# Moving a transpose's transfers to ScalarE's queue, and four turns of the result to an earlier stage, in a fused attention and mixer kernel

## The chip, the cores and the metric

The kernel runs on one core of a Trainium2 chip. A core has five engines that run their own instruction streams: TensorE (PE, matrix products; PEld is its loading of weights), VectorE (DVE), ScalarE (ACT), GpSimd (POOL) and SyncE (SP), which here only issues transfers. An engine's stream is in order: an instruction that waits holds everything behind it on that engine. Transfers are issued from an engine's queue and carried out by 16 DMA engines that all queues of the core share. Engines work on SBUF (128 partitions), matrix products end in PSUM, inputs and outputs lie in DRAM.

The metric is the device time of one execution in microseconds (us), the median of several runs.

## What is computed

Attention with normalised queries and keys over 8 batches, 12 heads, 448 positions and 64 numbers a head, then a token mixer and a channel mixer over the 768 channels of the joined heads (`q`, `k`, `v` are of shape (8, 12, 448, 64), the result is (8, 448, 768), all in float32):

```python
def rmsnorm(x, g):
    return x / np.sqrt(np.mean(x * x, axis=-1, keepdims=True) + 1e-06) * g
scores = 1.0 / np.sqrt(64) * np.matmul(rmsnorm(q, g_q), rmsnorm(k, g_k).transpose(0, 1, 3, 2))
attn = np.exp(scores - np.max(scores, axis=-1, keepdims=True))
attn = attn / (np.sum(attn, axis=-1, keepdims=True) + 1e-09)
x = np.matmul(attn, v).transpose(0, 2, 1, 3).reshape(8, 448, 768)
...
h = np.maximum(x.transpose(0, 2, 1) @ w_tok1, 0.0) @ w_tok2     # 448 -> 256 -> 448, over positions
u = x + h.transpose(0, 2, 1)
return u + np.maximum(u @ w_ch1, 0.0) @ w_ch2                   # 768 -> 1536 -> 768, over channels
```

## The kernel before

**The order of work.** Everything is one long program. The order on PE, DVE, ACT and POOL is the order in which the code emits instructions (`manual_schedule`, L49). The work is cut into items, each with a cost in us and a function that emits it. `merge` (L27) interleaves lists of items in proportion to their costs; `run` (L120) emits them and adds each cost to a software clock. `later(us, fn)` (L116) puts a piece of work, always the issue of a transfer, into a list of pending work; `run` emits it once the clock has passed the time asked for. Pending work is emitted first in, first out. This clock only orders instructions: on the chip each still waits for what it needs.

**The stages of a batch.** The mixer of batch b is interleaved with the attention of batch b+1: scores on PE (L334), exponentials on ACT (L338), values on PE (L408). The attention leaves x channel by channel, in `uT` (6 chunks of 128 channels, 448 positions each). For batch b the mixer then runs

1. `x_items`: the token mixing needs positions on the partitions. From batch 1 on x is turned round through DRAM: DVE transposes the 32x32 blocks of a chunk (L615), `send_x` (L581) writes each half of x (3 chunks) to a scratch `xs` in DRAM with four transfers of 168 KB, and `load_x` (L589) reads it back with one of 672 KB. All are issued by SP. The first half's turn lies among the attention's items, the second half's among the last four double products of the batch before (`last`, L971).
2. `tok1` (L623): four products of half of the channels, each of four matmuls (L629), each followed by a ReLU on ACT (L632). `h` is 0 for the first half of x, 1 for the second.
3. `tok2` (L634): six products, one for each chunk (L637), that DVE adds to `uT` (L642). `moving_sums` (L650) then forms the differences that the channel mixing uses.
4. `ch1` (L749): 3 x 7 products (L761) with sums on DVE, POOL and ACT. This and the next stage form 2x2 block products from seven multiplications in place of eight.
5. `ch2` (L803) in two groups: "double" products, for chunks 0, 1, 3 and 4 (14 items), then in `last_items` (L889) seven "single" products for chunks 2 and 5, each of 12 matmul records in the trace (L818). ACT copies the first product (L831), DVE and POOL add the others to `uT`. Batch 0 uses plain products (`ch1_first`, `ch2_first`).

**Weights.** The channel weights stream in as units of 384 KB (L687), in six buffers, up to five ahead, from SP's queue. A double product needs two units, a single one.

**The result.** The finished `uT` holds channels on the partitions, so it is turned too. For each of six chunks `trans_y` (L852) transposes blocks on DVE into a tile `turned` (four buffers, `turn_pool`, L89), and `send_y` (L574) writes it with four transfers of 56 KB, issued by ACT. For all batches but the last, all six turns are put into the token mixing of the next batch: `left[:2]` beside the first two `tok1` items, `left[2:]` beside the other two and the `tok2` items (L958 and L959). In the last batch four turns lie beside the single products.

**Waits between transfers.** In the built program every transfer signals on one of eight semaphores, taken in rotation in program order across the queues, and an issue first waits until the previous transfer on its semaphore has landed. The profile shows this as waits of one queue for another queue's transfer.

Of the kernel before, what the change touches and what calls it, by code (L numbers as in the profile page):

```python
# [26 lines left out]
def merge(*lists):  # L27

    totals = [sum(c for c, _ in l) or 1.0 for l in lists]
    done = [0.0] * len(lists)  # L30
    at = [0] * len(lists)
    res = []
    while True:
        live = [i for i in range(len(lists)) if at[i] < len(lists[i])]
        if not live:
            return res
        i = min(live, key=lambda i: (done[i] + lists[i][at[i]][0] / 2) / totals[i])
        c, fn = lists[i][at[i]]
        at[i] += 1
        done[i] += c  # L40
        res.append((c, fn))
# [3 lines left out]
def whole(ctx, tc, shifted, pre, q, k, v, g_q, g_k, moe_w_tok1, moe_w_tok2, moe_w_ch1, moe_w_ch2, out):  # L45


    nc = tc.nc
# [13 lines left out]
    NC = C // P  # L62
# [4 lines left out]
    KC, KF = NC // 2, NF // 2  # L67
# [46 lines left out]
    clock, pending = [0.0], []  # L114

    def later(us, fn):  # L116

        pending.append((clock[0] + us, fn))

    def run(items):  # L120
        for c, fn in items:
            fn()
            clock[0] += c
            while pending and pending[0][0] <= clock[0]:
                pending.pop(0)[1]()
# [70 lines left out]
    def sum_items():  # L196


        def one(i):
            n = len(stages)  # L200
            if i < n:
                t = st["sum", i] = raw_tile()
                nc.sync.dma_start(out=eight(t)[:, 0:4], in_=slots(i, 0, 4))
            if 0 <= i - 2 < n:
                q = eight(st["sum", i - 2])
                nc.gpsimd.tensor_tensor(out=q[:, 6], in0=q[:, 1], in1=q[:, 0], op=ALU.subtract)
                nc.gpsimd.tensor_tensor(
                    out=q[:, 4:6], in0=q[:, 1:7:5], in1=q[:, 3:4].to_broadcast([P, 2, P]), op=ALU.add)
                nc.gpsimd.tensor_tensor(out=q[:, 7], in0=q[:, 2], in1=q[:, 5], op=ALU.subtract)
            if 0 <= i - 3 < n:  # L210
                nc.sync.dma_start(out=slots(i - 3, 4, 8), in_=eight(st.pop(("sum", i - 3)))[:, 4:8])
                st["summed"] = i - 3 if i - 3 < n - 1 else n
                load_units(st["at"])

        def eight(t):
            return t[:].rearrange("p n w -> p (n w)").bitcast(F32).rearrange("p (q n) -> p q n", q=NQ)
        return [(1.0, lambda i=i: one(i)) for i in range(len(stages) + 3)]
# [356 lines left out]
    def send_y(b, cc, t):  # L574
        dst = out[b][:, cc * P:(cc + 1) * P]
        for i in range(0, P, 32):
            nc.scalar.dma_start(  # L577
                out=dst[:, i:i + 32].rearrange("(n t) c -> t n c", t=32),
                in_=t[i:i + 32].rearrange("t (n c) -> t n c", c=32))

    def send_x(b, half, t):  # L581

        xs = st["xs"] = xs_pool.tile([KC * S, P], F32, name="xs")
        for i in range(0, P, 32):
            nc.sync.dma_start(
                out=xs[:, i:i + 32].rearrange("(n t) c -> t n c", t=32),
                in_=t[i:i + 32].rearrange("t (n c) -> t n c", c=32))

    def load_x(b, half):  # L589
        nc.sync.dma_start(  # L590
            out=x_tile(b, half)[0:R].rearrange("p j c n -> p (j c) n"),
            in_=st.pop("xs")[:].rearrange("(g p) n -> p g n", p=R))

    def x_tile(b, half):
        st["x", b, half] = x_pool.tile([P, KC, NS, P], F32, name="x")
        return st["x", b, half]

    def trans_x(b, j):

        half, o = divmod(j, KC)  # L600
        if b == 0:

            if o == 0:
                x_tile(b, half)
            ps = s_tile("t_ps")
            for c in range(NS):
                nc.tensor.transpose(
                    ps[0:R, c * P:(c + 1) * P], st["uT", b][:, j, c * R:(c + 1) * R], ident[:, :])
            nc.scalar.copy(  # L609
                out=st["x", b, half][0:R, o], in_=ps[0:R, :].rearrange("p (c n) -> p c n", c=NS))  # L610
            return

        if j == 0:
            st["xt"] = tu_pool.tile([P, 2, KC, S], F32, name="xt", tag="tu")
        nc.vector.transpose(out=st["xt"][:, half, o, :], in_=st["uT", b][:, j, :])  # L615
        if o == KC - 1:
            t = st["xt"][:, half].rearrange("p j s -> p (j s)")
            if half:
                st.pop("xt")
            later(2.0, lambda: send_x(b, half, t))  # L620
            later(6.0, lambda: load_x(b, half))

    def tok1(b, jc, h):  # L623
        cs = slice(h * HC, (h + 1) * HC)
        if h == 0:
            st["h1", jc] = h1_pool.tile([P, C], F32, name="h1")
        ps = m_tile()
        for c in range(NS):
            nc.tensor.matmul(  # L629
                out=ps[:, 0:HC], lhsT=w1_sb[0:R, c, jc * P:(jc + 1) * P], rhs=st["x", b, h][0:R, :, c, :],  # L630
                start=(c == 0), stop=(c == NS - 1))
        nc.scalar.activation(out=st["h1", jc][:, cs], in_=ps[:, 0:HC], func=AF.Relu)  # L632
# [98 lines left out]
    def ch2_first(o, half, m):  # L731

        if half == 0:
            st["m", m] = m_tile()
        if m == 0:
            st["w"] = next_units(2)
        elif m == 2:
            st["w"] = next_unit()
        ps = st["m", m]
        for t in range(KF):  # L740
            w = st["w"][:, t // 2, t % 2, :] if m == 2 else st["w"][t // KC][:, t % KC, m, :]
            nc.tensor.matmul(  # L742
                out=ps[:, 0:S], lhsT=w, rhs=natural(half)[:, :, t, :],
                start=(half == 0 and t == 0), stop=(half == 1 and t == KF - 1))
        if half:
            u = st["uT", 0][:, o * KC + m, :]
            nc.vector.tensor_tensor(out=u, in0=u, in1=st.pop(("m", m))[:, 0:S], op=ALU.add)
# [101 lines left out]
        else:  # L849
            into(nc.vector, 1, 0, got)  # L850

    def trans_y(b, cc):  # L852

        t = turn_pool.tile([P, S], F32, name="turned")
        nc.vector.transpose(out=t[:], in_=st["uT", b][:, cc, :])
        later(2.0, lambda: send_y(b, cc, t))

    def turns(b, cs):
        return [(0.3, lambda cc=cc: trans_y(b, cc)) for cc in cs]

    us = lambda n, cols: n * cols * 4 / 2400

    def x_items(b, h):
        return [(0.1, lambda j=j: trans_x(b, j)) for j in range(h * NC // 2, (h + 1) * NC // 2)]

    def tok1_items(b, h):
        return [(us(NS, HC), lambda j=j, h=h: tok1(b, j, h)) for j in range(NJ)]
# [16 lines left out]
    def in_next(b):  # L884


        return b < B - 1 and not shifted

    def last_items(b, sums):  # L889

        single = [(us(6, HS), lambda i=i: ch2(b, 1, i, 0)) for i in range(7)]
        if b == 0:
            single = merge(
                [(us(6, S), lambda o=o, h=h: ch2_first(o, h, 2)) for o in range(2) for h in range(2)], sums)
        l = [] if in_next(b) else turns(b, [0, 1, KC, KC + 1])
        return [single[0]] + merge(single[1:-1], l) + [single[-1]]


# [50 lines left out]
    left, sums = [], sum_items()  # L949
    for b in range(B):  # L950
        early, double = middle_items(b)
        if b == 0:
            begin = x_items(0, 1) + tok1_items(0, 0) + tok1_items(0, 1)
            early = merge(begin + early, weight_items(BEFORE, then)) + merge(
                double, weight_items(then, len(chunks) + 3) + sums[:6])
        else:

            run(merge(tok1_items(b, 0), left[:2]))  # L958
            begin, early = merge(tok1_items(b, 1) + early[:3 * KC], left[2:]), early[3 * KC:]  # L959
            if b == 1:  # L960
                early, double = merge(begin + early, sums[12:33]), merge(double, sums[33:])
                begin = []
            early = begin + early + double
        lo = (b + AHEAD) * per + 1
        att = []
        if b + AHEAD < B:
            att = att_items(lo, lo + 10) + x_items(b + AHEAD, 0) + att_items(lo + 10, lo + per)
        tail = 4
        early, last = early[:-tail], early[-tail:]
        if b + 1 < B:  # L970
            last = merge(last, x_items(b + 1, 1))  # L971
        run(merge(att, early) + last + last_items(b, sums[6:12]))
        left = turns(b, range(NC) if in_next(b) else [2, KC + 2])
    run(left)
    for _, fn in pending:
        fn()
# [234 lines left out]
```

## Time and profile before

The time before is 1370.78 us, the median of three runs (1365.62 to 1374.34). The profiled execution has a span of 1375.2 us at a mean granted TensorE clock of 0.983.

| engine or queue | busy, us | share of the span |
|---|---|---|
| PE | 1297.2 | 94% |
| PEld (beside PE) | 930.2 | 68% |
| DVE | 758.0 | 55% |
| POOL | 397.1 | 29% |
| ACT | 389.5 | 28% |
| DMA, transfers issued by SP (225.97 MB) | | 64.5% of 16 engines |
| DMA, transfers issued by ACT (11.48 MB) | | 5.3% of 16 engines |

The issue of transfers isn't counted as busy time of an engine. A queue has its own rows in the views, such as SPq and ACTq. What matters for this change: 192 transfers `out_dram<-turned` from ACT, median 1.9 us from issue to landing; 56 `xs<-xt` from SP, 4.6 us; 14 `x<-xs` from SP, 7.1 us; 318 `unit<-ws` from SP, 4.0 us. A view of waits has one row for each pair of waiting line and releasing line; the releaser is inferred from semaphore events. A timeline has, for each row, the start, the duration in us, the engine, the line, the operation, the tiles as out<-in and the number of instructions joined, and in brackets the idle time ahead of it with its releaser.

### The profile page before, as it was taken

The page shows a single profiled execution, that of the slowest core. Times are in us where ns is not written, and L with a number is a line of the kernel's source. Part 1 is how long each engine was busy: PE and PEld are TensorE (multiplying, and loading weights), DVE is VectorE, ACT ScalarE, POOL GpSimd, SP SyncE. Part 2 cuts the span into 40 slices and gives each one's busy share as a digit, 9 for nine tenths or more (in the row PEclk, how much of TensorE's full clock was granted, in tenths as well). Part 3 has the DMA queues.
Part 4 walks back from the last instruction along what each step waited for, and adds up shares of the span by engine and source line. Part 5 has one row for each costly group of instructions (what it writes and reads, how often), then busy time and mean ns, then how long its engine had stood idle before and what let it go on. Part 6 is the DMA issues. An engine that isn't in the chain of part 4 may idle for free.

```text
span 1375.2 us, 20369 instructions
## 1 busy us (share of the span) xinstructions
PE 1297.2 (94%) x7408; PEld 930.2 (68%) x7408; DVE 758.0 (55%) x1300; ACT 389.5 (28%) x774; POOL 397.1 (29%) x386
## 2 busy tenths in 40 slices
PE   4888999989999999999999999999999989999996
PEld 2343444436687677785788667894887758787996
DVE  7978898217674365636574175634666155443212
ACT  6664544013330233203331133302432023300100
POOL 1213323346663242203330123312331023211220
PEclk9998999999999999999999999999999999999999
DMA  9684777998999666594658755594667846376655
GB/s 209 190 225 138 201 219 195 231 237 190 255 269 214 155 148 157 125 259 77 155 137 200 178 122 137 143 230 112 162 161 160 217 72 161 112 182 150 179 170 114
DMA packets 508147, 238.85 MB, mean 174 GB/s; under 512 B 374085, under 2 KB 466629, under 8 KB 508037
## 3 DMA queue, kind: packets, MB, share of 16 engines
q1 hardware_dynamic: 416962, 225.97, 64.5%
q10 hardware_dynamic: 90946, 11.48, 5.3%
q8 instruction: 61, 1.00, 0.3%
q14 instruction: 50, 0.40, 0.1%
q0 software_dynamic: 128, 0.00, 0.0%
HBM read 197.85 MB, written 39.52 MB: 173 GB/s over the span
## 4 chain that ended last, share of the span: by engine, by line
PE 74%; DVE 8%; DMA 7%; SPq 4%; issue 2%; ACT 2%; POOL 2%; ACTq 1%; DVEq 0%; POOLq 0%
PE m_ps L761 22%; PE m_ps L818 20%; PE s_ps L334 8%; PE o_ps L408 7%; PE m_ps L629 6%; PE m_ps L724 4%; DMA unit<-ws 3%; PE m_ps L742 3%; PE m_ps L637 2%; SPq L1071 1%; PE d_ps L388 1%; ACTq L577 1%; DVE es L376 1%; DMA ws<-raw 1%; DVE uT L642 1%
## 5 line engine op out<-in xcount | busy, mean ns | idle before, releaser
L818 PE MATMUL m_ps<-hb,unit 128*128 128x224 f32 x1764 | 347.8, 357 | 14.3 <-DMA unit<-ws 12.6
L818 PEld LDWEIGHTS m_ps<-hb,unit 128*128 128x128 f32 x1764 | 332.9, 191 | 34.7 <-issue 25.9
L761 PE MATMUL m_ps<-tu,unit 128*128 128x224 f32 x1008 | 201.6, 355 | 2.7 <-DVE hb L766 2.4
L761 PEld LDWEIGHTS m_ps<-tu,unit 128*128 128x128 f32 x1008 | 188.8, 190 | 18.6 <-issue 5.6
L338 ACT ACTIVATE e<-s_ps 128x448 f32<-128x448 f32 x336 | 157.2, 550 | 129.6 <-PE s_ps L334 94.1
L334 PE MATMUL s_ps<-qkT 64*64 64x448 f32 x1260 | 149.3, 560 | 3.8 <-ACT x L609 3.1
L761 PE MATMUL m_ps<-uT,unit 128*128 128x224 f32 x756 | 152.3, 355 | 0.3 <-DVE uT L642 0.3
L761 PEld LDWEIGHTS m_ps<-uT,unit 128*128 128x128 f32 x756 | 141.4, 190 | 14.8 <-DVE qkT L314 7.1
L408 PE MATMUL o_ps<-e,v 64*64 64x448 f32 x1316 | 150.0, 542 | 0.6 <-ACT uT L445 0.6
L827 POOL TENSOR_TENSOR uT<-uT,r 128x448 f32<-128x448 f32 (+1 forms) x56 | 50.6, 915 | 280.2 <-DVE r L827 149.0
L827 DVE TENSOR_TENSOR uT<-uT,m_ps 128x448 f32<-128x448 f32 (+1 forms) x70 | 33.8, 500 | 143.4 <-PE m_ps L818 143.4
L766 DVE TENSOR_TENSOR r<-m_ps,r 128x448 f32<-128x448 f32 x63 | 39.3, 623 | 131.1 <-PE m_ps L761 89.1
L376 DVE TENSOR_TENSOR es<-es,e 128x896 f32<-128x896 f32 x84 | 98.0, 1166 | 10.2 <-ACT e L338 7.3
L637 PE MATMUL m_ps<-w_sb,h 128*128 128x448 f32 x192 | 84.2, 580 | 19.1 <-DVE uT L642 15.9
L408 PEld LDWEIGHTS o_ps<-e,v 64*64 64x64 f32 x1316 | 50.2, 134 | 70.8 <-issue 64.3
L334 PEld LDWEIGHTS s_ps<-qkT 64*64 64x64 f32 x1260 | 44.2, 135 | 77.3 <-issue 63.0
L1104 DVE TENSOR_REDUCE ms<-sq 128x28 f32<-128x896 f32 (+2 forms) x47 | 51.3, 1091 | 80.7 <-ACT sq L1090 78.0
L766 POOL TENSOR_TENSOR hb<-r,r 128x448 f32<-128x448 f32 x21 | 23.9, 1136 | 225.0 <-ACT r L782 219.5
L629 PE MATMUL m_ps<-x,w_sb 112*128 112x384 f32 x256 | 88.2, 499 | 0.0
L260 POOL TENSOR_TENSOR stage<-raw 128x512 f32<-128x512 f32 x36 | 42.6, 1184 | 136.8 <-DVE raw L246 70.6
L637 PEld LDWEIGHTS m_ps<-w_sb,h 128*128 128x128 f32 x192 | 36.1, 197 | 63.2 <-DVE uT L642 30.1
L317 ACT ACTIVATE qkT<-qkT,g_t 128x448 f32<-128x448 f32 x36 | 24.0, 668 | 191.6 <-DVE qkT L314 191.6
(97 smaller groups left out, 1425.7 us busy)
## 6 DMA issues: line engine op xcount, KB each, us to landing
unit<-ws SPq DMA_DIRECT2D x318, 384.0 KB, 4.0
raw<-in_moe_w_ch_dram SPq DMA_DIRECT2D x72, 256.0 KB, 3.7
out_dram<-turned ACTq DMA_DIRECT2D x192, 56.0 KB, 1.9
v<-in_v_dram SPq DMA_DIRECT2D x94, 112.0 KB, 5.0
xs<-xt SPq DMA_DIRECT2D x56, 168.0 KB, 4.6
x<-xs SPq DMA_DIRECT2D x14, 672.0 KB, 7.1
ws<-stage SPq DMA_DIRECT2D x36, 256.0 KB, 3.8
raw<-ws SPq DMA_DIRECT2D x36, 256.0 KB, 4.6
```

The lines of the kernel that those rows point to most:

```text
L334: nc.tensor.matmul(out=pss[i][rows_of(i, a), 0:S], lhsT=qkT[h, 1, k * D:(k + 1) * D], rhs=qkT[h, 0, :], start=True, stop=True)
L338: nc.scalar.activation(out=e[:, i, :], in_=pss[i][:, 0:S], func=AF.Exp)
L376: eng.tensor_tensor(out=es[:], in0=(es if k > 1 else st["e", t, 0])[:], in1=st["e", t, k][:], op=ALU.add)
L408: nc.tensor.matmul(out=st["o", p][a * D:(a + 1) * D, 0:S], lhsT=vt[rows, k * D:(k + 1) * D], rhs=e[rows, :], **kw)
L629: nc.tensor.matmul(out=ps[:, 0:HC], lhsT=w1_sb[0:R, c, jc * P:(jc + 1) * P], rhs=st["x", b, h][0:R, :, c, :], start=(c == 0), stop=(c == N ...
L637: nc.tensor.matmul(out=ps[:, 0:S], lhsT=st["h1", jc][:, cc * P:(cc + 1) * P], rhs=w2_sb[:, jc].rearrange("p c r -> p (c r)"), start=(jc == ...
L724: nc.tensor.matmul(out=ps[:, 0:S], lhsT=st["w"][t // KC][:, t % KC, j, :], rhs=u[:, t, :], start=(t == 0), stop=(t == 2 * KC - 1))
L761: nc.tensor.matmul(out=ps[:, j * HS:(j + 1) * HS], lhsT=w[:, t, j, :], rhs=m, start=(t == 0), stop=(t == KC - 1))
L766: add = lambda e, o, x, y: e.tensor_tensor(out=o, in0=x, in1=y, op=ALU.add)
L818: nc.tensor.matmul(out=ps[:, j * HS:(j + 1) * HS], lhsT=st["w"](j, t), rhs=hb[:, HB[what], t, :], start=(t == 0), stop=(t == KF - 1))
L827: add = lambda e, o, x, y: e.tensor_tensor(out=o, in0=x, in1=y, op=ALU.add)
L1104: self.nc.vector.tensor_reduce(out=st["ms", p][:, p % 2, lo:hi], in_=sq[:, lo:hi], axis=AX_X, op=ALU.add)
```

## The change

Three edits belong together. First, the second half of x is sent to `xs` by ACT instead of SP, so that these four issues no longer stand between the weight units in SP's queue; its load back stays on SP and is put off longer. Second, four of the six turns of the result, those of the chunks that the double products have finished, move from the next token mixing to a place beside the single products; two are left. Third, the sends of these four turns are put off by 12 us of the software clock, so that they are emitted in the token mixing and not among the single products. Since put-off times now differ, the pending list is kept sorted by time.

```diff
     def later(us, fn):
-        pending.append((clock[0] + us, fn))
+        at = clock[0] + us
+        i = len(pending)
+        while i and pending[i - 1][0] > at:
+            i -= 1
+        pending.insert(i, (at, fn))
...
     def send_x(b, half, t):
-            nc.sync.dma_start(
+            (nc.scalar if half else nc.sync).dma_start(
...
             later(2.0, lambda: send_x(b, half, t))
-            later(6.0, lambda: load_x(b, half))
+            later(11.0 if half else 6.0, lambda: load_x(b, half))
...
-    def trans_y(b, cc):
+    def trans_y(b, cc, wait):
         t = turn_pool.tile([P, S], F32, name="turned")
         nc.vector.transpose(out=t[:], in_=st["uT", b][:, cc, :])
-        later(2.0, lambda: send_y(b, cc, t))
-
-    def turns(b, cs):
-        return [(0.3, lambda cc=cc: trans_y(b, cc)) for cc in cs]
+        later(wait, lambda: send_y(b, cc, t))
+
+    def turns(b, cs, wait=2.0):
+        return [(0.3, lambda cc=cc: trans_y(b, cc, wait)) for cc in cs]
...
-        l = [] if in_next(b) else turns(b, [0, 1, KC, KC + 1])
+        l = turns(b, [0, 1, KC, KC + 1], 12.0 if in_next(b) else 2.0)
         return [single[0]] + merge(single[1:-1], l) + [single[-1]]
...
-            run(merge(tok1_items(b, 0), left[:2]))
-            begin, early = merge(tok1_items(b, 1) + early[:3 * KC], left[2:]), early[3 * KC:]
+            run(merge(tok1_items(b, 0), left))
             if b == 1:
-                early, double = merge(begin + early, sums[12:33]), merge(double, sums[33:])
-                begin = []
-            early = begin + early + double
+                early, double = merge(early, sums[12:33]), merge(double, sums[33:])
+            early = tok1_items(b, 1) + early + double
...
-        left = turns(b, range(NC) if in_next(b) else [2, KC + 2])
+        left = turns(b, [2, KC + 2])
```

## Prediction

> **What bounds the kernel now.** I read the page first. TensorE (PE) is busy 1297.2 of 1375.2 us (94%) at a granted clock of 0.983, and the chain of work that ended last is 74% PE. The change alters no matrix product, so it can only return idle PE time, some 78 us, of which the first of the page's 40 slices, before all inputs are there, takes about 20. The list of what PE waits for names the part near this change:
>
> ```profile
> PE m_ps L637 <- DVE uT L642: 15.9, 9, 4.0
> ...
> PE m_ps L818 <- DMA unit<-ws: 12.6, 10, 2.5
> ...
> PE m_ps L637 <- ACT h L632: 3.2, 1, 3.2
> ```
>
> Columns: us in all, times, longest. L818 waits for the weight units of the last products of a batch, L637 for the token mixing. Both lie at the border between batches, where SyncE's queue (SP) issues units, x's way through DRAM (L585, L590) and the attention's loads. PE and SP at the border before batch 4:
>
> ```profile
> 755.02 9.32 PE L818 MATMUL m_ps<-hb,unit 128*128 128x224 f32 x48 [1.19 <-DMA unit<-ws]
> 764.55 4.78 PE L818 MATMUL m_ps<-hb,unit 128*128 128x224 f32 x24 [0.21 <-DMA unit<-ws]
> 771.79 4.02 PE L818 MATMUL m_ps<-hb,unit 128*128 128x224 f32 x12 [2.47 <-DMA unit<-ws]
> 775.61 4.58 PE L629 MATMUL m_ps<-x,w_sb 112*128 112x384 f32 x13
> ```
>
> ```profile
> 751.22 1.85 SPq L687 DMA_DIRECT2D unit<-ws  x4
> 753.16 6.17 SPq L585 DMA_DIRECT2D xs<-xt  x4
> 759.43 1.91 SPq L687 DMA_DIRECT2D unit<-ws  x2
> 762.30 0.32 SPq L590 DMA_DIRECT2D x<-xs  x1
> 762.72 4.69 SPq L687 DMA_DIRECT2D unit<-ws  x5
> ```
>
> The four L585 issues hold the queue 6.17 us; two units stand behind them, and the last single's unit stands behind the x load, which itself waits for xs to land. PE pays 1.19 + 0.21 + 2.47 = 3.9 us here. This was the end of batch 3. The same waits in the single products (the last seven of a batch) of the others, read from the same view: batch 1 0.69 + 2.31 = 3.0, batch 2 1.0, batch 4 1.7, batch 5 0.46 + 1.00 + 1.53 = 3.0, batch 6 none. They sum to the row's 12.6.
>
> Third, ScalarE (ACT) at the border from batch 2 to 3, because the sends of the result are issued there:
>
> ```profile
> 618.00 0.49 ACT L632 ACTIVATE h<-m_ps 128x384 f32<-128x384 f32 x1 [17.39 <-PE m_ps L629]
> 620.58 0.49 ACT L632 ACTIVATE h<-m_ps 128x384 f32<-128x384 f32 x1 [2.09 <-PE m_ps L629]
> 620.64 1.94 ACTq L577 DMA_DIRECT2D out_dram<-turned  x4
> 623.16 0.49 ACT L632 ACTIVATE h<-m_ps 128x384 f32<-128x384 f32 x1 [2.09 <-PE m_ps L629]
> 623.22 2.99 ACTq L577 DMA_DIRECT2D out_dram<-turned  x4
> 626.26 1.85 ACT L338 ACTIVATE e<-s_ps 128x448 f32<-128x448 f32 x4 [2.61 <-PE o_ps L408]
> ```
>
> ACT idles 17.39 us before the first ReLU, so ACT has free time during the single products; then four sends take 1.94 us (0.49 each). Last, DMA: in the windows of 595 to 605 and 605 to 615 us the 16 engines' mean busy share is 1.05 and 0.99, in 625 to 632 only 0.33. So the units of the single products also meet full DMA engines.
>
> **What the Trainium skill says.** "Trainium Kernel Development and Optimization", Key Constraints: the queues of SP, ACT and POOL run on the same 16 DMA engines, and issuing from several saves only the sequencer's issue time. The trace of before can't show it (no transfer of the same kind on two queues), but it sets my discount: x from ACT frees the 6.17 us of SP and no DMA time. "DMA: Bandwidth & Descriptors", Specifications, gives 512 B as the least transfer at full rate. The page agrees: the ACT queue moved 11.48 MB in 90946 packets (126 B each) for 5.3% of 16 engines' span, 12.8 ns a packet, 102 ps a byte; SP's 225.97 MB took 64.5%, 63 ps a byte. "Perfetto Trace Analysis", DMA Instruction — HWDGE: the profiled window of an issue is descriptor work and not data movement. The trace agrees: an L577 issue lasts 0.32 to 2.2 us (median 0.49), and the transfer lands after 1.9.
>
> **The change, part by part.** *x's second half from ACT.* Removed from SP: four issues of 6.2 to 7.7 us together at the end of each batch but the last; added to ACT in time it has idle. The units of singles 4 and 5 are issued up to 6 us sooner. The x load comes later (11.0 on the software clock for 6.0), so the last single's unit goes ahead of it; the second half of x is first read some 8 us after the token mixing starts (623 against 615), which covers the delay. Bounds: 0 if the full DMA engines set the landing, 12.6 if the queue does. xs (672 KB) now interleaves with the units of the first singles, and in the built order the copy of the first single (L831) stands behind the four xs issues on ACT. The program's DMAs signal on eight semaphores in rotation, and an issue first waits until the last transfer on its semaphore has landed; the fourth xs issue waits for the second's landing (xs<-xt: 2.6 to 8.6 us), so the copy is 1 to 2 us late; DVE's next sums follow it, PE has two PSUM tiles in hand. I take for the end of each batch: batch 1 0 (sums of the weights still share the queue there), batch 2 1, batch 3 3.5, batch 4 1.5, batch 5 2, batch 6 0: **8 us**.
>
> *Four turns beside the singles.* Four DVE transposes of 0.63 us move from the token mixing between the singles' additions. DVE is busy 1.19 and 1.68 us in the two ten-microsecond windows above, so 2.5 us fit: nothing on the path. The token mixing loses four transposes that sat between L642 additions. Only the border to batch 6 shows a large wait in which DVE's queue is held by the q and k norms of the attention (L637 waits 3.26 us); there the order now puts the L642 of the first chunk ahead of them: +2.4.
>
> *The sends put off.* There are four buffers of turned tiles, so the fifth and sixth turn wait for the first two turns' sends to land; all queue in ACT. In the built order ACT has four sends before the first ReLU, and 20 before the fourth ReLU, where before had 12. Behind the instruction on ACT stand the ReLUs and the exponentials of the attention. With 0.49 us each: third ReLU 623.2 to 625, exponentials 626.3 to 628.5, fourth ReLU 628.8 to about 630.6. PE's token product of chunk 3 (just after 629.8) needs the fourth ReLU, and waits some 1.2; part is won back in the attention that follows: −0.9 at the four borders from 1 to 2 up to 4 to 5, −3.6, and −1 at the border to batch 7, which has no attention to fill. Bounds: 0 and −3 a border.
>
> *The border from batch 0 to 1* is 39.75 us from its start to the first channel product where others have about 30. ACT idles 32.66 us before its first ReLU, then its first four sends hold ACT 7.44 us and exponentials wait 7.11 for a send's semaphore. The new order sends eight in the idle time: +5, bounds −1 and +11.
>
> Sum: 8 + 2.4 − 3.6 − 1 + 5 = **10.8 us**, 1370.8 − 10.8 = 1360.
>
> **Rivals.**
> A, *the queue was the whole limit*: all of 12.6, 7.4 at the first border, 2.4 at the border to batch 6, no loss in the token mixing: 22 us, 1349. For: SP is full between 751 and 767 us, and PE's last wait ends with a unit issued behind the x load. Against: DMA share 1.05.
> B, *transfers only take turns*: full DMA engines leave 4 of the 12.6, the first border gives 2, packed sends cost 1.5 at five borders: −1.5, so 1372. For: the DMA windows, 126-byte packets. Against: x's bytes are the same as before and only later.
> C, *ACT becomes the queue that stalls*: the xs issues hold the copy, so single products lose 3 us at six borders (18), the fourth ReLU is 1 us later on PE at seven borders (7), against 8 gained: +17, 1388. For: a shared semaphore already held SP up to 19.6 us behind out_dram. Against: ACT's idle 17 us ahead of the mixing.
>
> **How the numbers follow.** Main case 0.42, A 0.22, B 0.22, C 0.14. Around the main case I allow 8 us either side. Faster than 1357.1: A whole and a quarter of the main case, 0.33. Slower than 1384.5: most of C and a bit of B, 0.15. The rest, 0.52, is within 1%. Range: from a little under A, 1344, to the point where about half of C and nothing else is left out, 1384.
>
> **What would show it.** Right: the L818 wait for units falls from 12.6 to about 4.5; SP shows no L585 for the second half, and units follow units without a gap of 6 us; the border from 0 to 1 is near 35 us; L637 waits for h L632 appear, each about 1 us. If the L818 wait stays near 12 while the units are issued sooner, B's DMA limit holds. If PE waits at L818 for uT or for the copy's r, or ACT shows L585 issues of 2 us and more ahead of L831, C holds. The prediction is wrong above all if the rotation of semaphores ties an early ACT send to a late SP transfer (or the reverse), since that moves waits to places that I did not cost, or if the fourth ReLU is held longer than 2 us.

## The result

The changed kernel takes 1391.59 us (median of six, 1388.88 to 1397.59) against 1369.82 us for the kernel before (median of six): a ratio of 1.0165, interval 1.0134 to 1.0196. It is slower by 22 us, where 1360 us, 10 us less, had been predicted. Line numbers moved by 3 to 5: L577 is now L581, L585 is L590, L632 is L637, L637 is L642, L642 is L647, L687 is L692, L742 is L747, L761 is L766, L818 is L823, L831 is L836.

What PE waits for in the profile of the changed kernel, as (line <- releaser: us in total, times, longest):

```profile
PE m_ps L642 <- ACT h L637: 19.1, 8, 4.0
...
PE m_ps L823 <- DMA unit<-ws: 10.7, 5, 4.7
...
PE m_ps L642 <- DVE uT L647: 4.8, 3, 3.7
PE m_ps L766 <- DVE uT L647: 4.6, 5, 1.9
PE m_ps L747 <- DMA unit<-ws: 3.5, 2, 3.1
```

Read against the list of before: the largest wait is another one. The second token products waited 15.9 us for DVE's additions and 3.2 for a ReLU; now they wait 4.8 and 19.1. The single products' wait for units fell by only 1.9 us in all: at the ends of batches 2 to 5 it fell from 9.6 to 3.7 us, at the end of batch 1 it rose from 3.0 to 7.0. The last products of batch 0 (L747) wait 2.3 us more.

The best map is the length of each stage, from the starts of PE's first matmul of each stage in the timeline. I worked it out alike for every profile below. "Token" is from the first tok1 matmul to the first ch1 matmul, "ch1" the seven-product channel stage, "ch2" the double and single products.

| stage, us | before | changed | difference | predicted |
|---|---|---|---|---|
| ch2 of batch 0 | 62.39 | 68.00 | +5.6 | 0 |
| token of batch 1 (border 0 to 1) | 39.75 | 38.25 | −1.5 | −5 |
| ch2 of batch 1 | 63.58 | 67.19 | +3.6 | 0 |
| ch2 of batches 2 to 5 together | 247.42 | 239.56 | −7.9 | −8 |
| token of batches 2 to 5 together | 120.38 | 131.41 | +11.0 | +3.6 |
| token of batch 6 | 30.95 | 30.82 | −0.1 | −2.4 |
| token of batch 7 | 20.43 | 22.13 | +1.7 | +1 |
| ch1 of batches 1 to 7 together | 451.78 | 456.80 | +5.0 | 0 |

With −1.0 ahead of ch2 of batch 0 these make +16.5, the difference of the two profiles up to the last stage. The medians lie 22 us apart: the profiled execution of the kernel before took 1377.01 us, 7 more than its median. That goes with the granted clock: of the 56 executions of the kernel before beside some of the later runs, the 4 at a clock of 0.982 or 0.983 (the profiled one had 0.983) took 1375.6 us on average, the 17 at 0.988 or 0.989 took 1367.9. So stage tables against this one profile favour the other kernels by up to some 6 us, and a gain of one or two us in a stage isn't safe.

**Where the token mixing lost it.** ScalarE at the border from batch 2 to 3, the place shown for before:

```profile
606.11 7.34 ACTq L590 DMA_DIRECT2D xs<-xt  x4
613.54 0.35 ACT L836 COPY r<-m_ps 128x224 f32<-128x224 f32 x1 [14.81 <-DMA xs<-xt]
615.63 7.84 ACTq L581 DMA_DIRECT2D out_dram<-turned  x4
628.49 0.49 ACT L637 ACTIVATE h<-m_ps 128x384 f32<-128x384 f32 x1 [14.61 <-PE m_ps L634]
628.66 1.95 ACTq L581 DMA_DIRECT2D out_dram<-turned  x4
631.07 0.49 ACT L637 ACTIVATE h<-m_ps 128x384 f32<-128x384 f32 x1 [2.09 <-PE m_ps L634]
631.13 6.39 ACTq L581 DMA_DIRECT2D out_dram<-turned  x8
637.57 0.49 ACT L637 ACTIVATE h<-m_ps 128x384 f32<-128x384 f32 x1 [6.01 <-DMA out_dram<-turned]
637.60 4.29 ACTq L581 DMA_DIRECT2D out_dram<-turned  x8
641.93 1.85 ACT L342 ACTIVATE e<-s_ps 128x448 f32<-128x448 f32 x4 [3.87 <-DMA out_dram<-turned]
643.65 0.52 ACT L637 ACTIVATE h<-m_ps 128x384 f32<-128x384 f32 x1
```

Four sends stand ahead of the first ReLU and twenty more ahead of the fourth. The first four take 7.84 us, most of it waiting for SP's unit loads on the same semaphores, and cost nothing: the first ReLU waits for PE (L634), and it and the second come as long after the first token matmul as before. Between the second and the fourth ReLU stand 16 sends now, where 8 stood before (10 at this border). They take 6.39 + 4.29 = 10.7 us, and ACT idles 6.01 us ahead of the third ReLU, behind the first eight. The fourth ReLU starts 17.9 us after the first token matmul (643.65 less 625.71), where it was 13.6 (628.81 less 615.22): 4.3 us late. PE pays 3.91 us for it, and then runs 3.4 us at half the granted clock (645.5 to 648.9), which by this count adds some 1.7.

At the border from batch 3 to 4 no send is long:

```profile
794.27 4.12 ACTq L581 DMA_DIRECT2D out_dram<-turned  x8
```

Eight sends take 4.12 us, 0.5 each, and the fourth ReLU is 2.3 us late. At the four borders from 1 to 2 up to 4 to 5 it is 3.3, 4.3, 2.3 and 3.2 us late, and PE waits 2.4, 3.9, 1.6 and 2.3 us for it. In none of the four does a semaphore hold one of the 16 sends; the difference is a few single issues of 1.2 to 1.7 us. So here ScalarE's loss is the issue time of eight more sends, and not waiting for other transfers.

**Where the ends of batches 0 and 1 lost it.** The end of batch 0 on SP, ACT and PE:

```profile
258.45 8.23 SPq L692 DMA_DIRECT2D unit<-ws  x2
```

```profile
263.71 3.57 ACTq L590 DMA_DIRECT2D xs<-xt  x4
```

```profile
270.72 16.83 PE L747 MATMUL m_ps<-hb,unit 128*128 128x448 f32 x36 [3.06 <-DMA unit<-ws]
```

Two unit loads take SP 8.23 us. SP's waits over the whole execution tell why:

```profile
SPq L692 <- DMA xs<-xt: 29.4, 7, 7.4
```

The longest of these waits, 7.4 us, is the one here: SP's unit load waits from 258.96 to 266.33 us until x's transfer, now on ACT's queue, has landed. That transfer itself starts only at 263.71, when DVE has turned x. The two have a semaphore in common (117 in the trace), so work that waits in ACT's queue holds SP's queue. Before, this row did not exist. The row has a wait of 4.2 to 5.8 us at the end of each of batches 2 to 5 too, and there the stage gained all the same. At the end of batch 1 it is a load of keys that waits 3.1 us for x, with a unit behind it; PE's longest wait for a unit there is 4.75 us.

PE's waits for units explain only 2.3 of the 5.6 us that the end of batch 0 lost (1.2 before, 3.5 now). The rest is PE's own work at a lower granted clock. The stage before, the stage now, and a stretch of it (length, then busy time and number of instructions of PE, PEld, DVE, ACT and POOL, granted clock, DMA share, GB/s):

```profile
220.36:282.75 62.39, 61.19 (x212) 29.47 (x209) 29.48 (x51) 10.85 (x23) 18.79 (x28) 1.00 0.88 212
219.38:287.38 68.00, 64.49 (x212) 30.59 (x209) 31.62 (x55) 10.83 (x23) 20.43 (x31) 0.95 0.86 213
270.00:276.80 6.80, 6.08 (x8) 2.83 (x9) 0.00 (x0) 0.00 (x0) 2.11 (x5) 0.50 1.12 344
```

The same 212 matmul records are busy 3.3 us longer, and the 6.8 us at half clock begin where the wait of 3.06 us ends. It isn't the only such place. After the first 250 us of this trace each of PE's six waits of 3.1 us and more is followed by a stretch of 3.4 or 6.8 us at clock 0.50, and none of the shorter ones is; in the trace of before two waits of 2.3 and 2.5 us are followed by one too, so these traces give no sharp limit. A wait of PE can thus cost more than its own length.

**What was gained.** The single products at the end of batch 3, which had three waits of 3.9 us together, now have one:

```profile
765.67 4.70 PE L823 MATMUL m_ps<-hb,unit 128*128 128x224 f32 x24
772.89 16.13 PE L823 MATMUL m_ps<-hb,unit 128*128 128x224 f32 x84 [2.51 <-DMA unit<-ws]
788.85 3.39 PE L634 MATMUL m_ps<-x,w_sb 112*128 112x384 f32 x10
```

### The profile page after: what moved, and what is told of

Read it like the earlier page. It is cut to its first block, busy times and chain, and to the rows that moved or that the text cites. A ratio compares the mean times of both kernels' runs of the same rounds, so it can differ in the third digit from the quotient of the medians.

```text
span 1391.1 us, 20362 instructions
## 1 busy us (share of the span) xinstructions
PE 1300.5 (93%) x7408; PEld 930.1 (67%) x7408; DVE 766.4 (55%) x1300; ACT 388.8 (28%) x774; POOL 404.0 (29%) x386
## 4 chain that ended last, share of the span: by engine, by line
PE 78%; DVE 8%; DMA 5%; ACTq 3%; issue 2%; ACT 2%; SPq 1%; DVEq 0%
PE m_ps L766 24%; PE m_ps L823 21%; PE s_ps L338 8%; PE o_ps L412 7%; PE m_ps L729 4%; PE m_ps L747 4%; PE m_ps L642 4%; PE m_ps L634 4%; ACTq L581 3%; DMA unit<-ws 2%; DVE raw L231 1%; PE d_ps L392 1%; DVE es L380 1%; DVE qk_t L303 1%; DMA out_dram<-turned 1%
## 5 line engine op out<-in xcount | busy, mean ns | idle before, releaser
L823 PE MATMUL m_ps<-hb,unit 128*128 128x224 f32 x1764 | 344.0, 355 | 13.8 <-DMA unit<-ws 10.7
L823 PEld LDWEIGHTS m_ps<-hb,unit 128*128 128x128 f32 x1764 | 332.5, 191 | 31.0 <-issue 21.0
L766 PE MATMUL m_ps<-tu,unit 128*128 128x224 f32 x1008 | 201.9, 355 | 1.6 <-DVE r L771 1.6
L766 PEld LDWEIGHTS m_ps<-tu,unit 128*128 128x128 f32 x1008 | 188.7, 190 | 18.9 <-DVE r L771 4.8
L766 PE MATMUL m_ps<-uT,unit 128*128 128x224 f32 x756 | 152.1, 355 | 4.6 <-DVE uT L647 4.6
L766 PEld LDWEIGHTS m_ps<-uT,unit 128*128 128x128 f32 x756 | 141.5, 190 | 18.6 <-DVE uT L647 9.1
L642 PE MATMUL m_ps<-w_sb,h 128*128 128x448 f32 x192 | 84.6, 582 | 24.0 <-ACT h L637 19.1
L634 PE MATMUL m_ps<-x,w_sb 112*128 112x384 f32 x256 | 89.3, 504 | 3.2 <-ACT h L637 3.2
L771 POOL TENSOR_TENSOR hb<-r,r 128x448 f32<-128x448 f32 x21 | 27.6, 1314 | 210.3 <-ACT r L787 167.5
L642 PEld LDWEIGHTS m_ps<-w_sb,h 128*128 128x128 f32 x192 | 36.1, 199 | 69.3 <-issue 25.1
L380 POOL TENSOR_TENSOR es<-e 128x896 f32<-128x896 f32 x21 | 44.0, 2094 | 131.2 <-ACT e L342 131.2
```

Of the source, the lines that this page charges most:

```text
L380: eng.tensor_tensor(out=es[:], in0=(es if k > 1 else st["e", t, 0])[:], in1=st["e", t, k][:], op=ALU.add)
L634: nc.tensor.matmul(out=ps[:, 0:HC], lhsT=w1_sb[0:R, c, jc * P:(jc + 1) * P], rhs=st["x", b, h][0:R, :, c, :], start=(c == 0), stop=(c == N ...
L642: nc.tensor.matmul(out=ps[:, 0:S], lhsT=st["h1", jc][:, cc * P:(cc + 1) * P], rhs=w2_sb[:, jc].rearrange("p c r -> p (c r)"), start=(jc == ...
L766: nc.tensor.matmul(out=ps[:, j * HS:(j + 1) * HS], lhsT=w[:, t, j, :], rhs=m, start=(t == 0), stop=(t == KC - 1))
L771: add = lambda e, o, x, y: e.tensor_tensor(out=o, in0=x, in1=y, op=ALU.add)
L823: nc.tensor.matmul(out=ps[:, j * HS:(j + 1) * HS], lhsT=st["w"](j, t), rhs=hb[:, HB[what], t, :], start=(t == 0), stop=(t == KF - 1))
```

## The experiments

All ratios are against the kernel before on the same chip, with their 95% intervals.

**One part alone: x** (with the sorted pending list).

```diff
 (kernel before)
-            nc.sync.dma_start(
+            (nc.scalar if half else nc.sync).dma_start(
-            later(6.0, lambda: load_x(b, half))
+            later(11.0 if half else 6.0, lambda: load_x(b, half))
```

> Only the x edits (second half of x from ScalarE, its load back put off to 11, sorted pending list); all six turns stay in the next token mixing. Theory P (the sends packed ahead of the last ReLUs of the token mixing are the loss): the unit waits of the single products of batches 2 to 5 fall by about 8 us, the ends of batches 0 and 1 lose about 9 us because SyncE waits there for x's transfers, the token mixing is as before; 1366 to 1374 us. Rival X (x from ScalarE, through the shared semaphores, is the loss): 1385 us or more.

Measured: 1377.84 us, ratio 1.0042 (1.0027 to 1.0056). A small loss, between the two theories' times and nearer to the first. The stages decide: ch2 of batches 2 to 5 gain 10.8 us (236.67), ch2 of batch 0 and 1 lose 5.6 and 3.7 as in the whole change, and the token mixing of batches 2 to 5 stays at 30.0 us each. So x's move carries both the gain in the single products and the loss at the ends of batches 0 and 1, and nothing of the loss in the token mixing. These stages alone would make the kernel 1.5 us faster; in the medians it is 6 us slower, since the profiled execution of before lies 7 us above its median and this kernel's 2.5 below.

**One part alone: the turns.**

```diff
 (changed kernel)
-            (nc.scalar if half else nc.sync).dma_start(
+            nc.sync.dma_start(
-            later(11.0 if half else 6.0, lambda: load_x(b, half))
+            later(6.0, lambda: load_x(b, half))
```

> Only the turns and their put-off sends; x's second half stays on SyncE. Theory P: the token mixing of batches 2 to 5 keeps its waits for the fourth ReLU of 1.6 to 3.9 us each, the unit waits of the single products stay near 12 us; about 1380 to 1386 us. Rival X: 1368 to 1373 us, and no waits for the fourth ReLU over 1 us.

Measured: 1408.24 us, ratio 1.0252 (1.0226 to 1.0279). The turns alone cost 36 us; the time is 22 above theory P's range. PE waits 23.0 us for ReLUs in the second token products, as theory P had it, and the token mixing of batches 2 to 5 loses 13.4 us. But the waits for units in the single products are 19.3 us and not 12, and the ends of batches 0 and 1 lose 8.0 and 2.9 us though x goes from SyncE. The end of batch 0 takes 70.4 us, and here PE's wait and SP's are these:

```profile
PE m_ps L747 <- DMA unit<-ws: 7.2, 1, 7.2
```

```profile
SPq L692 <- DMA out_dram<-turned: 7.4, 1, 7.4
```

(both from the window of 219 to 291 us). Again SP's unit load waits for a transfer that waits in ACT's queue, this time a send of the result. Rival X falls.

**The sends not put off.**

```diff
 (changed kernel)
-        l = turns(b, [0, 1, KC, KC + 1], 12.0 if in_next(b) else 2.0)
+        l = turns(b, [0, 1, KC, KC + 1], 2.0)
```

> The whole change, but the four turns' sends are put off by 2 instead of 12: 16 sends (20 or so with x's) stand ahead of the first ReLU, in ScalarE's idle time, and 8 between the ReLUs. Theory P: the waits for the fourth ReLU vanish as far as the sends go out before the first ReLU; 1372 to 1380 us. Rival D (sends among the single products collide with the weight units on full DMA engines): unit waits above 15 us and 1390 us or more. Rival X: about 1390 us, as with the whole change.

Measured: 1405.00 us, ratio 1.0229 (1.0192 to 1.0266): slower than with the put-off, a miss for theory P as stated. The sends are not gone before the first ReLU:

```profile
620.71 18.83 ACTq L581 DMA_DIRECT2D out_dram<-turned  x16
639.59 0.49 ACT L637 ACTIVATE h<-m_ps 128x384 f32<-128x384 f32 x1 [20.62 <-DMA out_dram<-turned]
```

Sixteen sends take 18.83 us, and now the first ReLU stands behind them; PE waits 25.3 us in all at the first token products (L634). The sixteen issues themselves last 6.9 us together. The rest lies between them: 10 us of it ends when a unit load of SP or an earlier send on the same semaphore has landed. Rival D falls too, since the single products' unit waits are 7.9 us, less than with the put-off.

**The sends behind the ReLUs.**

```diff
 (changed kernel)
-        l = turns(b, [0, 1, KC, KC + 1], 12.0 if in_next(b) else 2.0)
+        l = turns(b, [0, 1, KC, KC + 1], 24.0 if in_next(b) else 2.0)
...
-            run(merge(tok1_items(b, 0), left))
+            run(tok1_items(b, 0) if not shifted else merge(tok1_items(b, 0), left))
+            if not shifted:
+                early[6:6] = left
```

(`shifted` is false in the program that was measured.)

> The whole change, but the four turns' sends are put off by 24 (all behind the fourth ReLU) and the last two turns move from the first token products to behind the token mixing's fourth second product. Theory P: no wait for the fourth ReLU beyond 0.5 us; what is left is x's part, 1366 to 1376 us. Rival X: 1385 us or more. Rival N (the token mixing loses wherever 24 sends stand on ScalarE, since exponentials and the norms wait instead): 1383 to 1392 us, with waits for exponentials in place of those for the ReLU.

Measured: 1399.82 us, ratio 1.0183 (1.0154 to 1.0213). The waits for ReLUs are gone (1.3 us once), and the kernel is no faster: rival N in kind. Its time is above N's range too, and the waits have not gone to the exponentials, as N had it, but here:

```profile
PE m_ps L642 <- DVE uT L647: 13.2, 8, 3.7
PE m_ps L766 <- ACT r L775: 10.3, 2, 5.5
...
PE m_ps L766 <- DVE uT L647: 9.5, 7, 1.9
```

Whatever stands behind the sends on ACT is late: here the squares and the small copies of the norms, and with them DVE's chain ahead of its additions (L647), and the channel stage's copy (L775). At the border from batch 2 to 3 a send holds the square for 1.6 us, and DVE sits idle for 15.6 us until that square is done.

**x from ScalarE for batches 3 to 7 only.**

```diff
 (the kernel with x alone)
-            (nc.scalar if half else nc.sync).dma_start(
+            (nc.scalar if half and b > 2 else nc.sync).dma_start(
-            later(11.0 if half else 6.0, lambda: load_x(b, half))
+            later(11.0 if half and b > 2 else 6.0, lambda: load_x(b, half))
```

> As the run with only the x edits, but x's second half goes from ScalarE only for batches 3 to 7; for batches 1 and 2, whose transfers share the end of the batch with the sums of the weights, it stays on SyncE. Theory S (an issue waits on a semaphore that the other queue's transfer still holds; at the ends of batches 0 and 1 that is x from ScalarE, and holds the weight units): the end of batch 0 (ch2 stage) falls from 68.0 back to about 62.4 us and that of batch 1 from 67.3 to about 63.6, the gains of batches 2 to 5 (10.7 us in the profile) stay; 1360 to 1367 us. Rival V (the ends of batches 0 and 1 vary from build to build, whatever the queue): both stay at 67 to 68 us and the time at 1374 to 1379.

Measured: 1365.91 us, ratio 0.9969 (0.9953 to 0.9985). ch2 of batch 0 is 62.0 us and of batch 1 63.0, as theory S said, and the granted clock in both is back at 1.00; ch2 of batches 2 to 5 keep 8.4 us of gain (239.00). Rival V falls. In this form the x part of the change is a small gain of 0.3%.

**All sends from SyncE.**

```diff
 (changed kernel, send_y)
-            nc.scalar.dma_start(
+            nc.sync.dma_start(
```

> The whole change, but every send of the result is issued by SyncE in place of ScalarE, at the same points of the software clock. Theory S: no ReLU and no exponential waits for sends any more, the waits for the fourth ReLU (19.1 us) vanish, and the token mixing is back at 30 us or less; SyncE has slack there (its units wait 230 us for free slots); 1372 to 1380 us, the rest being the ends of batches 0 and 1. Rival D (the sends' bytes on the DMA engines are the cost): 1388 us or more, as with ScalarE. Rival Q (24 sends of 0.5 us in SyncE's queue hold up units and q, k, v): unit waits above 20 us, 1390 us or more.

Measured: 1367.13 us, ratio 0.9983 (0.9969 to 0.9996), 24 us less than the changed kernel from one word, and better than expected. At the border from batch 2 to 3 the four ReLUs and the exponentials of ACT have no send ahead of them, and SP takes the sends in its slack:

```profile
625.62 0.49 ACT L637 ACTIVATE h<-m_ps 128x384 f32<-128x384 f32 x1 [2.09 <-PE m_ps L634]
626.55 1.85 ACT L342 ACTIVATE e<-s_ps 128x448 f32<-128x448 f32 x4 [0.44 <-PE s_ps L338]
630.81 0.49 ACT L637 ACTIVATE h<-m_ps 128x384 f32<-128x384 f32 x1 [2.41 <-PE m_ps L634]
```

```profile
615.48 17.91 SPq L581 DMA_DIRECT2D out_dram<-turned  x23
```

The token mixing of batches 2 to 5 takes 29.4 us each, less than before's 30.0. The bytes and the 192 transfers are the same, and so are their places on the software clock; rival D falls. Rival Q falls by its time, but something of it is there:

```profile
PE m_ps L766 <- DVE uT L647: 4.7, 5, 1.8
PE o_ps L412 <- DMA v<-in_v_dram: 4.4, 2, 2.8
```

PE now waits for v, whose loads stand in SP's queue, and ch1 of batch 1 takes 80.1 us (72.9 in the changed kernel). The other line is the wait of the first channel products for DVE. It is as long as in the changed kernel, with no send on ScalarE. ch2 of batches 0 and 1 stay at 68.1 and 66.4 us, the part of x.

**All sends from GpSimd.**

```diff
 (changed kernel, send_y)
-            nc.scalar.dma_start(
+            nc.gpsimd.dma_start(
```

> The whole change, but every send of the result is issued by GpSimd, whose transfers have semaphores of their own in the built program. Theory S: the waits for the fourth ReLU vanish and SyncE waits for no out_dram transfer; 1370 to 1380 us if GpSimd's issues cost about as much as ScalarE's. Rival G (issuing from GpSimd is slow, several us a send): GpSimd's sums are late and the time is 1400 us or more.

Measured: 1374.82 us, ratio 1.0028 (1.0015 to 1.0040), 17 us less than the changed kernel. A send costs GpSimd 0.63 us and counts as its busy time, 120.0 us in all:

```profile
L581 POOL DMA_DIRECT2D out_dram<-turned x192 | 120.0, 633 | 22.0 <-DVE turned L860 19.6
```

PE's waits for ReLUs are gone here too. SP's unit loads and q, k loads no longer wait for out_dram. One wait of 23.4 us of SP for a send is left (L1209); it is the one for the last sends at the end of the program, which the kernel before has too, with 17.2 us.

**Both losses taken away.**

```diff
 (the changed kernel with sends from SyncE)
-            (nc.scalar if half else nc.sync).dma_start(
+            (nc.scalar if half and b > 2 else nc.sync).dma_start(
-            later(11.0 if half else 6.0, lambda: load_x(b, half))
+            later(11.0 if half and b > 2 else 6.0, lambda: load_x(b, half))
```

> The sends from SyncE as in the run before but one, and x's second half from ScalarE only for batches 3 to 7. Theory S: both losses are gone; 1358 to 1368 us, faster than the kernel before. Rival Q (SyncE's queue gets too long): slower than 1372 us.

Measured: 1357.16 us, ratio 0.9913 (0.9895 to 0.9931). Both losses are undone, each by its own edit: ch2 of batch 0 is at 62.2 us and of batch 1 at 63.3, as with x alone for batches 3 to 7, and the token mixing of batch 1 at 27.6 (38.25 in the changed kernel, 39.75 before), as with the sends alone. ch1 of batches 1 to 7 stays 6.7 us above before.

**The kernel before, with sends from SyncE.**

```diff
 (kernel before, send_y)
-            nc.scalar.dma_start(
+            nc.sync.dma_start(
```

> The kernel before with one change: every send of the result is issued by SyncE in place of ScalarE; turns and x as before. If the queue of the sends is what matters and the place of the turns little, the token mixing of batches 1 and 6 falls to about 28 and 26 us as in the kernels with sends from SyncE, and the time to 1358 to 1365 us. If the moved turns are what then pays, it stays at 1367 to 1373 us: the sends would stand ahead of the units, and q and k, in SyncE's queue at the places where the first turns lay.

Measured: 1353.76 us, ratio 0.9883 (0.9864 to 0.9901): the fastest of the study. It is faster than both expectations. SP waits for no out_dram transfer any more, where in the kernel before four lines did, the largest with

```profile
SPq L1071 <- DMA out_dram<-turned: 74.9, 4, 19.1
```

The token mixing of batch 1 falls from 39.75 to 31.2 us and that of batch 6 from 30.95 to 27.6, less than was expected.

Four kernels make a square (in ratios, since the chips differ). The sends on ScalarE cost 16 us in the kernel before (1.0000 against 0.9883) and 25 in the changed one (1.0165 against 0.9983). So most of what the sends cost was there before the change, and the change added some 9. With the sends on SyncE the change still costs 14 us, of which x at two borders is 10 (0.9983 against 0.9913).

**The same with x from ScalarE for batches 3 to 7.**

```diff
 (the kernel with x for b > 2, send_y)
-            nc.scalar.dma_start(
+            nc.sync.dma_start(
```

> Sends from SyncE, x's second half from ScalarE for batches 3 to 7, but all six turns in the next token mixing as before. Against the run with both and moved turns (1357 us): the same within 3 us if the place of the turns is worth little, 1362 us or more if moving the four turns pays once the sends are off ScalarE.

Measured: 1355.94 us, ratio 0.9903 (0.9889 to 0.9917). Against 0.9913 with the moved turns the intervals overlap: no gain of moving the four turns can be seen once the sends are off ScalarE. They overlap with the run above too: the gain of x's move, visible alone, does not show on top of it.

## Why the prediction was wrong

Two steps failed above all: x's cost on the other queue, which stood at nothing and was 9.2 us at the ends of batches 0 and 1, and the loss in the token mixing of batches 2 to 5, which stood at 3.6 us and was 11.0.

- *x from ScalarE, gain in the single products: right in kind, and in size partly by luck.* 8 us were named for batches 2 to 5, 7.9 came; one by one 1.0, 2.9, 1.3 and 2.7 against 1, 3.5, 1.5 and 2. PE's waits for units there fell by 5.8 us (9.6 to 3.7; to 1.3 with x alone), and its waits for DVE's sums rose by 1.6. Another 3.3 us are PE's busy time, half of it at the end of batch 3, where the granted clock was 0.98 in the profile of before and 1.00 in the other.
- *x from ScalarE, its cost: the step that was left out.* The prediction knew that an issue waits for the last transfer on its semaphore, and followed it one way, within ACT ("so the copy is 1 to 2 us late"). The other way was left out: SP's loads wait for x's transfer in ACT's queue, which waits for DVE. The end of batch 1, taken as 0, was +3.6, and that of batch 0, not named at all, +5.6. Sending x from SyncE for these two borders took both away, where x was moved alone and where the sends were on SyncE. The sentence on what would make the prediction wrong, an early ACT send tied to a late SP transfer "or the reverse", had it, at no price.
- *The sends put off, −3.6 and −1: right in kind, wrong in size.* The four borders cost 11.0 us for 3.6, the border to batch 7 1.7 for 1. The price of 0.49 us a send was nearly right (the median in the changed kernel is 0.50). The count, 20 sends ahead of the fourth ReLU against 12, is 24 against 8 (10 at the border shown) in the traces, but eight of these stand ahead of the second ReLU, where at these borders they delay nothing, so the eight more that were reckoned with are what counts. What was too small is the result: the fourth ReLU was to be 1.8 us late and is 2.3 at best, 4.3 at worst; PE was to wait 1.2 us and waits 1.6 to 3.9; and nothing was won back in the attention that follows. The stated bound, 3 us a border, was passed at the border shown (5.1), and so was the sign named for this, a fourth ReLU held longer than 2 us.
- *The ch1 stages were left out.* They lost 5.0 us. PE's first channel product waits for DVE's last addition (L647), 4.6 us in five times. The late fourth ReLU isn't the cause: the wait is 4.7 us in five times with the sends on SyncE, where no ReLU is late, and the two kernels with sends on SyncE and the turns in their old place have 0.3. So it comes with the moved turns; by which order on DVE was not tested.
- *The border from 0 to 1: +5 was hoped for, +1.5 came.* Eight sends did move ahead of the first ReLU, and took 11.24 us there; the next four take 7.13, of which 5.8 end with landings of SP's loads, and the first token products now wait 3.2 us for a ReLU that they had not waited for. The 7.44 us that the prediction gave to the first four sends of before were those of the second four; the first four took 2.36.
- *The border to batch 6: +2.4, measured +0.1.* The wait for DVE's addition (3.3 us) went, and one for the fourth ReLU (3.5) took its place. The prediction had charged no sends at this border.
- *Rival C, ScalarE becomes the queue that stalls, with 1388 us, was the nearest*, and had 0.14. Its end is right and half of its mechanism: the ReLUs are late. The other half, that the copy behind x's transfers costs 3 us at six borders, did not come: the single products of batches 2 to 5 got faster.

One reading of the prediction does not hold for every batch: x's four issues at a batch's end take 4.9 us in batch 0 and 4.0 in batch 6, outside its 6.2 to 7.7.

What stays open: no run changed the semaphores alone, so the price of sharing them rests on the waits in the traces and on moving transfers to other queues. The turns alone cost 14 us more than turns and x together. The single products account for 12 of that (ch2 of batches 2 to 5: 251.54 against 239.56 us). That the losses at the ends of batches 0 and 1 don't add up when both parts are there fits one queue held by whichever transfer of the other comes last, but was not tested by itself.

## What to carry to other kernels

A transfer issued from a compute engine's queue stands in that engine's program order, and whatever it waits for, data or a semaphore shared with another queue, everything behind it waits for too: here a ReLU started only after sixteen sends that took 18.83 us. Before moving a transfer to "an idle engine", list what stands behind it there, and, in the other direction, which issues of the other queues wait for its semaphore until its data exist. Price a packed run of issues as their number times the median, count those that stand between the two instructions that matter, and add what each can wait for. And try the plainest queue first: all sends from SyncE, which had slack, made the kernel before 1.2% faster with no other change.

## What the runs showed that was not expected

- An issue costs the same in company: four sends of the result took 1.94 us where they stood alone in the kernel before, eight packed ones 4.12. Where eight took 6.39 us, two single issues were long (1.74 and 1.27 us); where sixteen took 18.83, most was waiting for landings on shared semaphores.
- The same 192 sends at the same places of the program cost 25 us more on ScalarE than on SyncE, where PE waits 4.4 us for v instead. GpSimd lay between: 0.63 us of its own busy time for each.
- Taking a wait for the ReLUs away gave nothing while the sends stayed on ScalarE: the waits went on to the norms, DVE's additions and the copies.
- A longer wait of PE is paid again in granted clock: 2.3 us of waits at the end of batch 0 came with 3.3 us of slower matmuls.
